# Decode block, forward and backward: row results as rows, and the query weight transposed as work of its own

## The chip, the cores and the metric

The kernel runs on one core of a Trainium2 chip. The metric is the device time of one execution in microseconds (us), the median of several. Lower is better.

## What is computed

The reference is the gradient step of a decode block for two tokens. Its forward part normalises `x`, adds an attention over a cached key/value store and a gated product network without activation function, and the backward part returns the gradients by every input but `B_x`:

```python
# B=2, Sq=1, D=576, Hq=32, Hkv=16, Sk=4096, Dh=128, F=4608, all bf16
def _A_ref(x, k_cache, v_cache, wq, wo):
    q = (x @ wq).reshape(B, Sq, Hq, Dh).transpose(0, 2, 1, 3)
    k, v = (jnp.repeat(c, 2, axis=1) for c in (k_cache, v_cache))
    p = softmax(jnp.einsum("bhqd,bhkd->bhqk", q, k) * Dh ** -0.5)
    o = jnp.einsum("bhqk,bhkd->bhqd", p, v)
    return o.transpose(0, 2, 1, 3).reshape(B, Sq, Hq * Dh) @ wo
def _B_ref(x, w_gate, w_up, w_down):
    return ((x @ w_gate) * (x @ w_up)) @ w_down
xn = layernorm(x)
out = x + _A_ref(xn, k_cache, v_cache, wq, wo) + _B_ref(xn, w_gate, w_up, w_down)
# outputs: out, and the vjp of out with grad_out: dx, dk, dv, dwq, dwo, dw_gate, dw_up, dw_down
```

`out_0` is the forward result and `out_1` is dx, two rows of 576 numbers each. `out_2` and `out_3` are the gradients of the caches, 32 MiB each. The others are the weight gradients.

## The kernel before

All inputs are read once and all outputs written once: some 92 MB each way.

**Steps and groups.** The 32 pairs of a batch row and a key/value head are worked through in 16 steps of two heads. Two steps (the two batch rows) make a group `g`, with a slice of 512 columns of `wq` and 512 rows of `wo`. A step loads two k and two v tiles of 1 MiB (`load_kv`), transposes them on DVE (`turn`), and computes the scores (L1268), the softmax, the contraction with v or k (L1442) and the outer products that are the gradients of v and k (`head_outer`, L1290; "pp" belongs to dv, "dd" to dk). `group_front` computes q and the gradient of the attention's output. `group_back` adds the group's part of the forward result to `acc`, and its part of the gradient by xn to `accx`. It also starts the units for the gradients of `wo` (`rows_unit`, L727) and of `wq` (`cols_unit`, L713, and `wide_unit`, L764, each with a tail of 64 rows, L826). `mlp` does the same for the nine slices of F.

**A unit** is a handful of products into a PSUM tile of two banks (`o`, three of them) and an eviction to a store tile on ACT or DVE (L470, L472). When all units of a store tile are done, `put` issues its store on SP (L696). All large loads and stores are issued by SP, which takes them in order and waits for each one's data and slot.

**Slots.** 16 tiles of 1 MiB (`big`) are shared by loaded tiles (`kv`), transposed ones (`X`), store tiles (`st`) and gate/up slices (`G`), each with a cap. There are five `ww` tiles for slices of `wq`, `wo` and `w_down`, and two PSUM tiles `m` of one bank for all small products.

**The order** of the instructions on every engine is fixed when the kernel is built. Generators yield what they need (`PE(...)`, `DVE(...)`, `ACQ` for a slot, `WAIT` for events). A planner (`Order`) advances them by estimated costs and takes, among those that are ready within `SLACK`, the one with the lowest priority number from `pr`. Tables of constants (`OFF`, `HEAD`, `TAIL`, `PR`, `MLP_AT`, `WQ_AT`, `WO_AT`) make these numbers, one for each kind of work and step.

**The ends of the rows.** `acc` holds the forward result in columns, 128 partitions by five pieces by two rows. `final_out` turns it into rows with nine fp32 products (L1504, L1507) behind two bf16 products that add `x` (`rows_add`, L1490). `rows_put` evicts with ACT and DVE and stores `out_0` with one DMA (L1486). `accx` holds partial sums of the gradient by xn, 144 columns on 128 partitions. `final_dx` sums it into columns with F8 (L1521, L1522), does the layer norm's gradient in columns with a mean product (L1530), adds `grad_out` (L1490), and turns the columns into rows with eight fp32 products (L1540, L1543). `front` prepares the columns of normalised `x` (`xnT`) with twenty small products (L650, L653).

Of the kernel before, what the change touches and what calls it, by code (L numbers as in the profile page):

```python
# [13 lines left out]
P = 128  # L14
# [276 lines left out]
def DMA(engine, cost, nbytes, row=8192):  # L291
# [7 lines left out]
OFF = {"turn0": {0: -1015.2, 1: -14.6, 2: -608.5, 3: -352.4, 4: -44.2, 5: -609.4, 6: 1026.5, 7: -575.3, 8: -336.9,  # L299
       9: -48.1, 10: 73.1, 12: 183.6, 13: 1140.9, 15: 354.0}, "turn1": {0: -158.8, 1: 373.8, 2: -399.3, 3: -123.5,  # L300
       4: -561.8, 5: 1792.7, 6: 184.6, 7: -225.4, 8: -1188.5, 9: -525.0, 10: -1211.4, 11: -134.5, 12: 1399.2, 13:
       -786.3, 14: 125.3, 15: -889.4}, "att": {0: -320.6, 1: 25.1, 2: -524.3, 3: 1437.6, 4: -1231.0, 5: 704.1, 6:
       -946.7, 7: -1656.2, 8: -1046.6, 9: 659.5, 10: -617.2, 11: -169.8, 12: 46.5, 13: -31.6, 14: -222.6, 15:
       1033.5}, "dsc": {0: -1811.3, 1: -9.9, 2: 131.1, 3: 301.3, 4: -3.2, 5: 235.2, 6: -975.3, 8: 26.8, 9: 229.2,
       10: -420.4, 11: 210.0, 12: 19.1, 13: 299.2, 14: 9.4}, "conv": {0: -2015.6, 1: 231.3, 2: -0.4, 3: -50.3, 4:
       -1165.8, 5: 1061.5, 6: 135.8, 7: 373.5, 8: -2359.6, 9: 3.5, 10: 1574.4, 11: 172.6, 12: 216.0, 13: 448.3, 14:
       255.6, 15: 10.6}, "con": {0: -32.2, 1: 1152.5, 2: 1696.5, 3: 720.8, 4: 638.1, 5: 104.8, 6: -260.9, 7: -158.3,
# [3 lines left out]
       9: -103.2, 10: -395.3, 11: 2850.9, 12: 125.0, 13: 2376.4, 15: -25.5}, "front": {0: -90.0, 1: 2844.9, 2:  # L311
       -805.5, 3: -966.7, 4: 1527.3, 5: 109.2, 6: 51.9, 7: -924.3, 8: -171.1, 9: -1466.9, 10: -796.2, 11: 95.0, 12:
       407.0, 13: 194.7, 14: 42.9, 15: -116.8}, "back": {0: -1180.5, 1: 591.1, 2: -2708.2, 3: 979.9, 4: 556.1, 5:
# [7 lines left out]
       13: -595.2, 14: -250.1, 15: 5.1}, "mlp": {0: 248.5, 1: 1168.1, 2: -620.3, 3: -398.1, 4: -321.8, 5: 2002.0, 6:  # L321
       162.1, 7: -3.7, 8: -33.1, 9: -2.4, 10: 1014.3, 11: 985.4, 12: 835.4, 13: -9.7, 14: 314.7, 15: -413.5},
       "load": {0: 1074.9, 1: -427.7, 2: 2940.0, 4: -302.0, 5: 501.3, 6: 157.2, 7: 2723.0, 8: 41.7, 9: 175.7, 10:
       -1207.2, 11: -514.7, 12: -5.8, 13: 248.9, 14: 607.8, 15: -253.7}, "wload": {0: -271.1, 1: 208.8, 2: -1828.2,
       3: 108.3, 4: 438.0, 5: -390.0, 6: 623.3, 7: 89.8, 8: -357.2, 9: -50.4, 10: 1806.6, 11: 48.4, 12: -1247.3, 13:
       3030.4, 14: 857.3, 15: 1037.7}, "mload": {0: 867.2, 1: -358.1, 2: -1319.2, 3: 100.2, 5: 58.5, 6: -3446.8, 9:
       -71.5, 10: -371.1, 11: -312.3, 12: 9.2, 13: 247.9, 14: 253.2, 15: -7.2}}
MLP_AT = [1.14, 5.4, 2.05, 2.45, 26.26, 69.69, 14.36, 0.0, 155.88]
WQ_AT = [-126, 9, 14, 22, -10, -36, 47, 13]
WO_AT = [-81, -88, -157, -95, 31, 1, -2, -56]  # L330
# [3 lines left out]
BIAS = 0.188  # L334
SLACK = {"PE": 0.06, "ACT": 0.25, "DVE": 0.4, "POOL": 10000.0, "SP": 10000.0}
STEP = 28.0
HEAD = {"turn0": -995.0, "turn1": -3790.2, "att": -3348.0, "dsc": 396.0, "conv": -832.5, "con": 1401.5, "out1":
        -1892.2, "out0": 2828.7, "front": 21.6, "back": 291.8, "W0": -1455.9, "W1": -155.0, "BD1": 1364.6, "BD0":
        2903.1, "mlp": 2389.4, "load": -3080.4, "wload": 394.7, "mload": -742.1}
TAIL = {"turn0": 3370.1, "turn1": 9221.8, "att": 665.4, "dsc": 359.0, "conv": 2694.5, "con": 2347.7, "out1": 7925.6,  # L340
        "out0": -1730.3, "front": 756.2, "back": 2986.8, "W0": 3398.4, "W1": -331.2, "BD1": -2581.8, "BD0": -508.7,
        "mlp": -5065.9, "load": 6824.2, "wload": 208.6, "mload": 3569.7}
PR = {"turn0": 1475.9, "turn1": 1614.7, "att": -4652.5, "dsc": -2890.4, "conv": 226.3, "con": -1413.1, "out1":
      3893.4, "out0": 2308.0, "front": 679.0, "back": 881.2, "W0": -1279.8, "W1": -624.6, "BD1": 2069.1, "BD0":
      -1551.4, "mlp": -735.6, "wout": -435.6, "store": -3305.7, "load": -1982.4, "wload": -3953.8, "fin": 5877.7,
      "const": 11595.3, "mload": -2275.6}
# [8 lines left out]
def kernel(  # L355
# [121 lines left out]
    nmu = const.tile([2, 1], FP32, name="nmu")  # L477
    warm = const.tile([1, 1], FP32, name="warm")
    rstd = const.tile([2, 1], FP32, name="rstd")
# [11 lines left out]
    meanc = filled("meanc", [P, 1], FP32, 1.0 / D)  # L491
    xnT = filled("xnT", [P, 16], FP32, 0.0)
    nrT = const.tile([P, 4], FP32, name="nrT")
    gg = const.tile([P, 2, 16], FP32, name="gg")
    gp4 = const.tile([P, 4], FP32, name="gp4")
    zero1 = filled("zero1", [P, 1], FP32, 0.0)
    acc = filled("acc", [P, 5, 2], FP32, 0.0)
# [17 lines left out]
    F8 = const.tile([P, 8], FP32, name="F8")  # L515
    Q4 = const.tile([P, 4], FP32, name="Q4")
# [1076 lines left out]
```

## Time and profile before

| | |
|---|---|
| median of 3 runs | 465.89 us (465.81 to 466.47) |
| profiled execution | 465.85 us, of which the span is 464.1 us |
| PE, DVE, ACT, POOL busy | 80%, 79%, 73%, 31% of the span |
| DMA | 185.97 MB, 401 GB/s over the span |
| mean granted PE clock | 0.70 of full speed |
| the 91 large stores (1024 and 576 KB), from issue to landing | 14.0 and 11.0 us (medians) |

The span is the time from the first to the last instruction of the profiled execution. Busy shares are averages over the whole span. An engine's busy time counts only where it ends last. The DMA line is the bytes that the 16 DMA engines moved. A line such as L470 is a helper's line: all plain evictions on ACT bear it, so the tile names say which work it was.

### The profile page before, as it was taken

The numbers are of one execution on the slowest core, as the hardware profiler recorded it, in microseconds if no ns is written. First come the engines' busy times: TensorE is split into PE (matmuls) and PEld (weight loads), VectorE is DVE, ScalarE is ACT, GpSimd is POOL, SyncE is SP. The second block draws the span as 40 slices with busy tenths as digits, with TensorE's granted clock in tenths as the row PEclk, the third lists the DMA queues.
The fourth block names the chain that finished last, engine by engine and source line by source line (L and its number), as shares of the span: only waits on it lengthen the run. The fifth ranks groups of instructions, "written<-read, shape, count | busy, mean of one in ns | idle before, by whom it ended". The sixth has DMA issues, their size and how long they took to land. (4 is left out here: it accounts for less than half of the span.)

```text
span 464.1 us, 15709 instructions
## 1 busy us (share of the span) xinstructions
PE 372.6 (80%) x6750; PEld 213.9 (46%) x6750; DVE 366.2 (79%) x708; ACT 337.7 (73%) x515; POOL 143.1 (31%) x174
## 2 busy tenths in 40 slices
PE   1677779789986877887887788879888987976995
PEld 1444455546443444454555354644543442533543
DVE  8897888876779887778987688977966887877782
ACT  3278639868886787765867778858857987897973
POOL 0740043303316443460016251140344463053000
PEclk9978776965557676756775796755666676586955
DMA  8999999999999999999999999999999999999994
GB/s 312 416 409 422 410 426 395 408 414 372 355 415 422 407 422 407 411 423 425 414 405 418 419 423 420 424 414 411 400 406 395 394 422 424 424 404 349 422 384 186
DMA packets 40710, 185.97 MB, mean 401 GB/s; under 512 B 3640, under 2 KB 12352, under 8 KB 24256
## 3 DMA queue, kind: packets, MB, share of 16 engines
q1 hardware_dynamic: 40632, 184.96, 98.7%
q8 instruction: 53, 0.87, 0.7%
q14 instruction: 17, 0.14, 0.1%
q10 hardware_dynamic: 8, 0.00, 0.0%
HBM read 92.48 MB, written 92.48 MB: 399 GB/s over the span
## 5 line engine op out<-in xcount | busy, mean ns | idle before, releaser
L470 ACT CAST big<-ps_o 128x1024 bf16<-128x1024 f32 (+2 forms) x309 | 278.9, 963 | 50.6 <-PE ps_o L1290 23.8
L466 DVE STREAM_TRANSPOSE big<-big 128x1024 f32<-128x1024 f32 x146 | 176.4, 1223 | 18.3 <-DMA big<-in_A_v_cache_dram 8.4
L1256 POOL TENSOR_TENSOR BD<-vr,mask 128x2048 bf16<-128x2048 bf16 x32 | 115.2, 3603 | 121.6 <-DVE vr L472 49.1
L472 DVE CAST big<-ps_o 128x1024 bf16<-128x1024 f32 (+1 forms) x69 | 73.4, 1065 | 17.8 <-PE ps_o L764 7.7
L1268 PE MATMUL ps_m<-big,W 128*32 128x128 bf16 x2048 | 57.3, 272 | 4.3 <-issue 1.8
L1233 POOL COPY W<-rep 32x16 bf16<-32x16 bf16 x128 | 24.6, 192 | 115.2 <-DVE rep L1007 99.2
L1268 PEld LDWEIGHTS <-W 128*32 128x32 bf16 x2048 | 45.5, 121 | 23.5 <-issue 22.5
L1290 PE MATMUL ps_o<-BD,dd 32*128 32x512 bf16 x256 | 45.8, 523 | 9.2 <-ACT big L470 5.6
L1290 PE MATMUL ps_o<-BD,pp 32*128 32x512 bf16 x256 | 44.5, 465 | 9.1 <-ACT big L470 7.5
L466 DVE STREAM_TRANSPOSE big<-ww 128x1152 f32<-128x1152 f32 (+1 forms) x25 | 33.0, 1318 | 3.5 <-DMA out_dram<-big 3.4
L1442 PE MATMUL ps_m<-big,dd 128*32 128x512 bf16 x256 | 30.7, 578 | 1.6 <-DVE dd L466 0.9
L1442 PE MATMUL ps_m<-big,pp 128*32 128x512 bf16 x256 | 29.2, 545 | 3.5 <-DVE pp L466 2.8
L1290 PEld LDWEIGHTS <-pp 32*128 32x128 bf16 x256 | 10.3, 95 | 29.3 <-issue 25.0
L1290 PEld LDWEIGHTS <-dd 32*128 32x128 bf16 x256 | 10.7, 99 | 26.3 <-issue 18.7
L764 PEld LDWEIGHTS <-xnr 32*128 32x128 bf16 x368 | 13.6, 119 | 14.3 <-issue 13.3
L764 PE MATMUL ps_o<-D,xnr 32*128 32x128 bf16 x256 | 14.7, 285 | 4.9 <-ACT big L470 3.6
L727 PE MATMUL ps_o<-dyr,R 32*32 32x288 bf16 x256 | 17.8, 406 | 0.8 <-ACT big L470 0.7
L1039 POOL COPY qr<-qd 128x256 bf16<-128x256 bf16 x8 | 3.2, 395 | 45.8 <-DVE qd L472 43.1
L727 PE MATMUL ps_o<-dyr,hb 32*32 32x288 bf16 x288 | 15.4, 327 | 1.7 <-ACT big L470 1.6
L888 PE MATMUL ps_m<-big,Wdy 128*128 128x128 bf16 x162 | 16.2, 278 | 0.4 <-DVE cr L1394 0.3
L678 PE MATMUL ps_m<-big,wm 128*32 128x128 bf16 x416 | 13.7, 294 | 2.6 <-DVE cr L1394 1.2
L888 PEld LDWEIGHTS <-Wdy 128*128 128x128 bf16 x162 | 14.4, 127 | 3.0 <-issue 2.7
(206 smaller groups left out, 481.6 us busy)
## 6 DMA issues: line engine op xcount, KB each, us to landing
out_dram<-big SPq DMA_DIRECT2D x74, 1024.0 KB, 14.0
big<-in_A_k_cache_dram SPq DMA_DIRECT2D x32, 1024.0 KB, 14.9
big<-in_A_v_cache_dram SPq DMA_DIRECT2D x32, 1024.0 KB, 13.6
out_dram<-big SPq DMA_DIRECT2D x17, 576.0 KB, 11.0
ww<-in_B_w_down_dram SPq DMA_DIRECT2D x9, 576.0 KB, 13.1
ww<-in_A_wo_dram SPq DMA_DIRECT2D x8, 576.0 KB, 10.9
ww<-in_A_wq_dram SPq DMA_DIRECT2D x8, 512.0 KB, 10.7
big<-in_B_w_gate_dram SPq DMA_DIRECT2D x4, 1024.0 KB, 14.5
```

Of the source, the lines that this page charges most:

```text
L466: nc.vector.transpose(out, in_)
L470: nc.scalar.copy(out, in_)
L472: nc.vector.tensor_copy(out=out, in_=in_)
L678: nc.tensor.matmul(dp[32 * q:32 * q + 32, 0:P], lhsT=W, rhs=view(X, 0, P, xoff(q, s), [[FS, 4], [2, 32]]), start=(s == 0), stop=(s == S - 1))
L727: nc.tensor.matmul(o[32 * q:32 * q + 32, aa, 0:HD2], lhsT=view(t, 32 * q, 32, 2 * A + aa, [[4, 32]]), rhs=dyr[32 * q:32 * q + 32, k * HD2: ...
L764: nc.tensor.matmul(o[:, aa, j * P:(j + 1) * P], lhsT=xnr[32 * a:32 * a + 32, dc * P:(dc + 1) * P], rhs=rhs(a), start=True, stop=True)
L888: nc.tensor.matmul(dh, lhsT=Wdy[:, e, 2 * k:2 * k + P], rhs=view(X[:], 0, P, 64 * k + e, [[D, FC], [2, 32]]), start=(k == 0 and e == 0), s ...
L1233: nc.gpsimd.tensor_copy(view(W_t[t][w][:], 32 * a, 32, 6 + 8 * a, [[G * WW, 4], [WW, G], [1, 2]]), view(rep_t[grp[g]["qs"]][:], 32 * a, 32 ...
L1256: nc.gpsimd.tensor_tensor(BD_t[i][:], view(vr_t[v][:], 0, P, 0, [[0, 16], [1, Dh]]), view(mask16[:], 0, P, 0, [[1, 16], [0, Dh]]), ALU.mult)
L1268: nc.tensor.matmul(sc[32 * cq:32 * cq + 32, :], lhsT=view(W[:], 0, P, (be * G + l) * WW + 6 - 4 * c2 - 2 * l, [[1, 32]]), rhs=view(X[:], 0 ...
L1290: nc.tensor.matmul(o[:, k, :], lhsT=pr2[32 * c4:32 * c4 + 32, :], rhs=BD[32 * c4:32 * c4 + 32, 8 * l + 4 * h2:8 * l + 4 * h2 + 4, :], star ...
L1442: nc.tensor.matmul(ct[32 * j:32 * j + 32, :], lhsT=view(rT, 0, P, 4 * c + 2 * l, [[1, 32]]), rhs=kv_t[kvS[s][t][l]][:, Dh * c:Dh * (c + 4) ...
```

## The change

Three things change together.

1. **Rows.** `acc` changes its layout from pieces by rows to rows by pieces, so that one fp32 product with the identity gives ten rows of 128 numbers: `final_out` is that product, one DVE addition of `x` (kept in the same form, `xrow`), and four stores. `final_dx` sums `accx` into eight rows of 144 numbers with one product, does the layer norm's gradient on DVE in that form (with one small product for the means), and stores it with three DMAs whose pieces are 64 and 32 bytes long. `front` prepares `x` and `grad_out` in these forms with 21 bf16 products and one fp32 product. `final_out` has a priority of its own (`finy`).
2. **Transposes of `wq`.** The two DVE transposes of a group's `wq` slice leave `group_back` and form a generator of their own, `turn_wq`, with priorities `wqt`. It waits for the group's `Ed` and for the `spread` of its second step, takes an `X` slot, and gives the `ww` tile back. `group_back` waits for `Ewqt`.
3. **The order.** All tables of constants are new, and `BIAS` and `SLACK` (the planner's preference of ACT for evictions, and its window of choice) with them. The planner's other costs are as they were.

The diff without the tables:

```diff
-BIAS = 0.188
-SLACK = {"PE": 0.06, "ACT": 0.25, "DVE": 0.4, "POOL": 10000.0, "SP": 10000.0}
+BIAS = 0.117
+SLACK = {"PE": 0.06, "ACT": 0.26, "DVE": 0.32, "POOL": 10000.0, "SP": 10000.0}
...
-    acc = filled("acc", [P, 5, 2], FP32, 0.0)
+    acc = filled("acc", [P, 2, 5], FP32, 0.0)
...
     # front(): preparation of the row forms
-            for c in range(4):
-                nc.tensor.matmul(tp[32 * c:32 * c + 32, 2 * a:2 * a + 2], lhsT=xb[:, P * c + 32 * a:P * c + 32 * a + 32],
-                                 rhs=ident[0:2, 0:2], start=True, stop=True)
...
+        for dc in range(5):
+            nc.tensor.matmul(tp[0:10, 288:416], lhsT=Zw[:, 4 - dc:14 - dc], rhs=xb[:, DOFF[dc]:DOFF[dc] + P],
+                             start=(dc == 0), stop=(dc == 4))
...
+        for n in range(2):
+            row = xy[0:2, n * D:(n + 1) * D]
+            for a in range(4):
+                nc.tensor.matmul(tp[0:8, 144 * n:144 * n + P], lhsT=Zw[:, 3 - a:11 - a],
+                                 rhs=view(row, 0, 2, 32 * a, [[P, 4], [1, 32]]), start=(a == 0), stop=(a == 3))
...
+        nc.vector.tensor_copy(xrow, tp[0:10, 288:416])
+        nc.vector.tensor_copy(grow, tp[0:8, 144:288])
+        nc.vector.tensor_copy(nr8, tp[0:8, 416:418])
+        nc.vector.tensor_scalar(xn8, tp[0:8, 0:144], nr8[:, 0:1], nr8[:, 1:2], op0=ALU.add, op1=ALU.mult)
+        nc.vector.tensor_scalar(nrs, nr8[:, 1:2], -1.0, None, op0=ALU.mult)
...
+    def turn_wq():
+        for g in range(NG):
+            st = grp[g]
+            yield PRIO(pr("wqt", 2 * g))
+            yield WAIT(st["Ed"], steps[2 * g + 1]["spread"])
+            wq = ww_t[st["wq"]]
+            x = st["wqt"] = yield ACQ("X")
+            X = X_t[x]
+            yield DVE(1.25)
+            t32(pairs(X[:, 0:4 * FS]), pairs(wq[:, 0:4 * FS]))
+            yield REL("ww", st["wq"])
+            yield DVE(0.4)
+            t32(pairs(X[:, 4 * FS:5 * FS]), pairs(tq[:, FS * (g % 4):FS * (g % 4 + 1)]))
+            yield SET(st["Ewqt"])
...
     # group_back(g)
-        x = yield ACQ("X")
+        yield WAIT(st["Ewqt"])
+        x = st["wqt"]
         X = X_t[x]
-        yield DVE(1.25)
-        t32(pairs(X[:, 0:4 * FS]), pairs(wq[:, 0:4 * FS]))
-        yield REL("ww", st["wq"])
-        yield DVE(0.4)
-        t32(pairs(X[:, 4 * FS:5 * FS]), pairs(tq[:, FS * (g % 4):FS * (g % 4 + 1)]))
...
     def final_out():
-        yield PRIO(PR["fin"])
+        yield PRIO(PR["finy"])
         yield WAIT(Eprep, *acc_E)
-        i = yield ACQ("o")
...
-        yield from rows_put(o, 0, out_0)
-        yield REL("o", i)
+        i = yield ACQ("m")
+        yt = m_t[i][0:10, 0:P]
+        yield PE(0.0, 0.4)
+        nc.tensor.matmul(yt, lhsT=acc[:].rearrange("p b k -> p (b k)"), rhs=identf[:], start=True, stop=True)
+        yield DVE(0.25)
+        nc.vector.tensor_tensor(yrow, yt, xrow, ALU.add)
+        yield REL("m", i)
+        rows = out_0.rearrange("b s d -> (b s) d")
+        for b in range(2):
+            yield DMA("SP", 0.3, 1024, 256)
+            nc.sync.dma_start(rows[b, 0:512].rearrange("(c n) -> c n", c=4), yrow[5 * b:5 * b + 4, :])
+            yield DMA("SP", 0.3, 128, 128)
+            nc.sync.dma_start(rows[b:b + 1, 512:576], yrow[5 * b + 4:5 * b + 5, 64:P])
 
     def final_dx():
...
+        g8, mt = m_t[i][0:8, 0:144], m_t[i][0:8, 144:146]
+        yield PE(0.0, 0.5)
+        nc.tensor.matmul(g8, lhsT=F8[:], rhs=accx[:], start=True, stop=True)
+        yield DVE(0.6)
+        nc.vector.reduce_sum(s8[:, 0:1], g8, axis=AX.X)
+        nc.vector.tensor_tensor_reduce(out=t8, in0=xn8, in1=g8, scale=1.0, scalar=0.0, op0=ALU.mult, op1=ALU.add,
+                                       accum_out=s8[:, 1:2])
         yield PE(0.0, 0.1)
+        nc.tensor.matmul(mt, lhsT=M8[:], rhs=s8, start=True, stop=True)
+        yield DVE(0.9)
+        nc.vector.tensor_copy(m8, mt)
+        nc.vector.scalar_tensor_tensor(out=t8, in0=xn8, scalar=m8[:, 1:2], in1=g8, op0=ALU.mult, op1=ALU.subtract)
+        nc.vector.tensor_scalar(t8, t8, m8[:, 0:1], nrs, op0=ALU.add, op1=ALU.mult)
+        nc.vector.tensor_tensor(dxrow, t8, grow, ALU.add)
+        yield REL("m", i)
+        rows = out_1.rearrange("b s d -> (b s) d")
+        for b in range(2):
+            yield DMA("SP", 0.3, 1024, 64)
+            nc.sync.dma_start(rows[b, 0:512].rearrange("(c a j) -> a c j", a=4, j=32),
+                              dxrow[4 * b:4 * b + 4, 0:P].rearrange("a (c j) -> a c j", j=32))
+        yield DMA("SP", 0.3, 256, 32)
+        nc.sync.dma_start(rows[:, 512:576].rearrange("b (a j) -> b a j", a=4), dxrow[0:8, P:144])
```

More of the change, by code (lines that the diff above doesn't have):

```diff
@@ L655, in front @@
-        nc.tensor.matmul(bp, lhsT=view(ones[:], 0, 2, 0, [[0, P]]), rhs=nr, start=True, stop=True)
-        yield DVE(0.9)
-        nc.vector.tensor_copy(xnT[:, 0:8], tp[:, 0:8])
-        nc.vector.tensor_copy(xnT[0:16, 8:16], tp[0:16, 8:16])
-        nc.vector.tensor_copy(nrT[:], bp)
-        for k, op in ((0, ALU.add), (2, ALU.mult)):
-            nc.vector.tensor_tensor(xnT[:], xnT[:], view(nrT[:], 0, P, k, [[0, 8], [1, 2]]), op)
-        nc.vector.memset(gg[:, 0], 0.0)
+        tp = m_t[i]
@@ new lines, in front @@
+        yield PE(0.0, 0.6)
+        for dc in range(5):
+            nc.tensor.matmul(tp[0:10, 288:416], lhsT=Zw[:, 4 - dc:14 - dc], rhs=xb[:, DOFF[dc]:DOFF[dc] + P],
+                             start=(dc == 0), stop=(dc == 4))
+        yield DVE(0.2)
+        nc.vector.memset(Zw[:], 0.0)
+        nc.vector.tensor_copy(view(Zw[:], 0, 2, 3, [[4, 2]]), ident[0:2, 0:2])
+        yield PE(0.0, 1.2)
+        for n in range(2):
[3 more added lines that the diff above has]
+                                 rhs=view(row, 0, 2, 32 * a, [[P, 4], [1, 32]]), start=(a == 0), stop=(a == 3))
+            for a in range(4):
+                nc.tensor.matmul(tp[0:8, 144 * n + P:144 * n + 144], lhsT=Zw[:, 3 - a:11 - a],
+                                 rhs=row[:, 512 + 16 * a:528 + 16 * a], start=(a == 0), stop=(a == 3))
@@ L971, in mlp @@
         yield REL("hb", hs)
[L974 removed]
+    grp = [dict(Lm=Event(), Eq=Event(), Ed=Event(), Lo=Event(), EoT=Event(), Ewqt=Event()) for _ in range(NG)]
     Lq = events(2)
@@ L1527, in final_dx @@
-        nc.vector.tensor_tensor(gx, g, xnT[:], ALU.mult)
-        nc.vector.reduce_sum(gp4[:], view(gg[:], 0, P, 0, [[16, 2], [1, 2], [2, 8]]), axis=AX.X)
-        yield PE(0.0, 0.1)
-        nc.tensor.matmul(mt[:, 16:20], lhsT=view(meanc[:], 0, P, 0, [[0, P]]), rhs=gp4[:], start=True, stop=True)
-        yield DVE(0.5)
-        mean = [view(mt[:], 0, P, 16 + 2 * k, [[0, 8], [1, 2]]) for k in range(2)]
-        nc.vector.tensor_tensor(gx, xnT[:], mean[1], ALU.mult)
-        nc.vector.tensor_tensor(gx, g, gx, ALU.subtract)
```

179 lines of the change are left out of this document (68 added, 111 removed), and 21 rows, old and new, of the table OFF.

## The prediction, made before the changed kernel was run

> **What bounds the kernel now.** I read the page's slices first, then the busy time by stretch, then SP's issues in order of time, then the chain that ended last.
>
> ```profile
> PEclk9978776965557676756775796755666676586955
> DMA  8999999999999999999999999999999999999994
> GB/s 312 416 409 422 410 426 395 408 414 372 355 415 422 407 422 407 411 423 425 414 405 418 419 423 420 424 414 411 400 406 395 394 422 424 424 404 349 422 384 186
> ```
>
> The 16 DMA engines are busy nearly throughout, at 400 to 426 GB/s, and the bytes do not change. So time is lost only where these engines run dry. The last slice (186 GB/s) is the largest such place. The stretches show the others (columns: us, busy time and count on PE, PE weight loads, DVE, ACT and POOL, granted clock, DMA share, GB/s):
>
> ```profile
> 112.00:114.00 2.00, 2.00 (x54) 1.43 (x48) 1.59 (x4) 1.99 (x3) 0.09 (x1) 0.50 0.67 263
> 418.00:420.00 2.00, 1.17 (x37) 0.71 (x35) 0.00 (x0) 2.00 (x3) 0.00 (x0) 1.00 0.61 232
> 448.00:450.00 2.00, 2.00 (x25) 0.93 (x25) 1.49 (x5) 1.44 (x2) 0.00 (x0) 0.50 0.76 281
> 456.00:458.00 2.00, 1.11 (x10) 0.71 (x5) 0.69 (x4) 1.01 (x1) 0.00 (x0) 0.50 0.30 91
> 460.00:462.00 2.00, 0.00 (x0) 0.00 (x0) 0.03 (x1) 0.26 (x1) 0.00 (x0) 0.50 0.08 29
> ```
>
> One minus the DMA share, times the length, is idle time. Over 112 to 116 it is 0.66 + 0.48 = 1.1 us, over 416 to 420 0.16 + 0.78 = 0.9 us: some 2.1 us in mid-kernel. From 446 to the end, in the same 2 us stretches, it is 0.48 + 0.20 + 1.40 + 0.40 + 1.84 + 2.03 = 6.4 us. In that tail PE works without a pause at half clock (6.00 of 6.00 us between 448 and 454; ACT 3.07, DVE 3.30). PE is therefore late there, and the stores with it:
>
> ```profile
> 449.29 0.56 PE ps_o L1490 x2
> 449.86 1.80 PE ps_o L1504 x16
> 451.65 0.30 PE ps_o L1507 x2
> 451.95 1.08 PE ps_o L727 x12
> ...
> 454.46 0.53 PE ps_m L1521 x2
> 454.99 0.15 PE ps_m L1522 x2
> 455.14 0.56 PE ps_o L1490 x2
> 455.70 0.54 PE ps_o L713 x8
> ...
> 457.65 1.87 PE ps_o L1540 x8
> ```
>
> This is the chain (start, us, what). The products of `final_out` stand ahead of the rows units (L727) that feed the last three large stores, and the first products of `final_dx` stand between the two units (L713) of the very last one.
>
> ```profile
> 457.32 0.38 SPq L696 DMA_DIRECT2D out_dram<-big  x1
> 460.29 0.26 SPq L1486 DMA_DIRECT2D out_dram<-xy  x1
> ```
>
> The last line is `out_1`, issued last. It does not end last: SP's final wait (L1588) is put down to `out_dram<-big`, 2.3 us, and by the packet records `out_1` is moved at 461.0 while the last 1 KB piece of the large store ends at 462.7, 1.4 us before the end. So the store issued at 457.32 sets the end, and a shorter `final_dx` gains nothing unless that store also comes earlier.
>
> **The change, part by part.** Sums are made against the profiled execution, 465.85 us = span 464.07 + 1.78, which is the median (465.89) but for 0.04.
>
> *`final_out` on PE.* Removed: 0.56 + 1.80 + 0.30 = 2.66 us. Added: one fp32 product of 128 columns; the four such products of L1540 take 1.87 us, so 0.47 each. The removed work lies on the path to the last store: -2.19 us.
>
> *`final_dx` before its last unit.* 0.53 + 0.15 + 0.56 = 1.24 us stand between the two last units. In the new order the F8 product comes behind all sixteen products of these units: -1.24 us. Together the last large store moves by 3.43 us, from 457.32 to 453.9.
>
> *What is late next.* DMA: the stretches from 446 on move 4.52 MB, which at 415 GB/s take 10.9 us; with 1.4 us to the end that floor is 458.3, below 464.07 - 3.43 = 460.64. ACT and DVE are half idle there. So the store stays the end.
>
> *The rest of `final_dx`.* It must end below 460.64. The last units now end on PE at 456.24 - 3.43 = 452.8; DVE evicts its half of the last store first (1.2 us), to 454.0. Then a reduction over 144 columns (0.30, as the 128x144 add L1111), the multiply with sum (0.29 + 0.08, L1386), the fp32 mean product (0.53, L1530), a copy (0.15), three passes over 144 columns (0.35 as L1397, then 0.30 and 0.27) and 0.3 for seven hand-overs of 0.02 to 0.05: 2.6 us, to 456.6. Three issues of 0.3 us: the third begins at 457.2. Its packets follow 0.75 us later (460.29 to 461.05 now), and 1.4 us close: 459.4. Hidden, by 1.2 us; beyond that it costs its excess.
>
> The trace holds no store in 64 and 32 byte pieces; its nearest row is the 1152 byte row at 0.05 us a packet, against 0.009 us for a 4 byte semaphore write, so 40 pieces on 16 engines cost 0.03 to 0.15 us. The Trainium skill (DMA: Bandwidth & Descriptors, Specifications) says that transfers under 512 B are read, modified and written, and its latency section gives up to 2 us for one access under load. By that, as an estimate, `final_dx` would end at 461.4 instead of 459.4 and the time would be 463.2; no row here shows it, and the sum does not use it.
>
> The PE terms are taken at the tail's granted 0.50. The Trainium skill (TensorE: Matmul & The Clock Gate, What's actually happening) says that 3.4 us of sustained work release full clock. The trace disagrees: PE is busy 6.00 of 6.00 us at 0.50. By the rule the removed work would be worth about half, 1.7 us, and the time 464.1.
>
> *Four stores for `out_0`.* Three more SP issues, 0.9 us, ahead of the last three large stores. SP is idle between 452.75 and 453.81, which covers them; uncovered, +0.9.
>
> *Preparation.* DVE has 12 small instructions in place of 11, two of them wider (0.3 each): +0.5 us between 12 and 17 us, before waits for PE of 0.68, 0.56 and 0.26 us, while the queue holds loads only (first store at 30.22). Zero; uncovered, +0.5.
>
> *`turn_wq`.* The same transposes (1.2 + 0.40 us a group), taken out of `group_back` and put ahead. In the tail they run at 449.6 to 451.2, with the product that needs them at 452.96: not on the path, so zero. It holds one of the 16 big slots for longer; a load that then waits is late by about a transpose, up to 1.6 us.
>
> *The order.* SP's first 17 loads are the same in both orders. After that all differs. By SP's list, the last v load stands 1.0 MiB later (162.2 behind 161.2), about 2.5 us, and 14.2 MiB follow it instead of 15.2. PE has by then done more: behind the last dp scores 6 instead of 14 pp products (L1290, 0.30 each) and none instead of 16 (L1442, 0.12 each) remain, 4.4 us less. That covers the 2.5 us. The first of the last dK stores stands 9.3 MiB (23.5 us) behind that load, 12.0 before; from the landing (by 423.04) to that store (about 446) it took 23 us, so the cover is thin. Over the other steps the least such distances are 10.0 and 11.2 (before 12.9 and 13.2), 25 us and more. For mid-kernel I take no change; its bounds are -2.1 us (all idle gone) and the loss of the second rival.
>
> Sum: 465.85 - 2.19 - 1.24 = 462.4 us.
>
> **The rivals.** *More than the tail:* the new order also loses the idle of 112 to 116 and 416 to 420: 462.4 - 2.1 = 460.3. For it: the fourth gate/up slice is spread out (its down load stands at 42.1 MiB, not 31.4), and the first stall came in a stretch where PE was busy 6.00 of 6.00. Against: every order so dense must stall somewhere.
>
> *Slower:* SP takes its queue in order, so a store whose evictions are late holds up the loads behind it, and once DMA's backlog of about 10 us (14 us to landing less 4 for an empty queue, my estimate) is spent, DMA runs dry. Before, two wide stores of `grads` took SP from 111.0 to 117.0, and DMA lost 1.1 us. In the new order four of them stand in a row, two v loads behind them, and only 10.0 MiB after the down load they depend on (12.0 before). At the same pace they take 12 us, 6 us more with the backlog already spent: 462.4 + 6 = 468.4. It decides from 4.4 us of added idle. Against: the slice's PE work is no longer bunched with the three others.
>
> *It does not reach the end:* the last store's path shortens, but a later v load, thin cover at the last dK stores or a straggling DMA engine gives 3 us back: about 465.4.
>
> **How the numbers follow.** A difference of under 0.2% (0.93 us) can't be told from no change. Forecast, 461 to 464.5: 0.50. More than the tail: 0.15. Given back: 0.11. Slower: 0.24. Faster is 0.65, same 0.11, slower 0.24. The range goes from 459.0 (the first rival, and 1.3 for the spread of DMA rates) to 468.5 (the second).
>
> **What would show it.** Right: `final_out` one product of about 0.5 us; from the last rows units to the last large store no fp32 products on PE; idle DMA after 446 of about 3 us; SP's last wait still for `out_dram<-big`. Wrong: a slice in mid-kernel under 340 GB/s, above all around the four wide stores in a row; or SP's last wait for `out_dram<-xy`, which would mean that the small pieces end last; or a tail in which PE idles and evictions or loads are late.

## Result and profile after

The changed kernel takes 471.53 us (median of 6 runs, 470.41 to 471.73) beside 466.39 us for the kernel before on the same chip (6 runs, 465.81 to 466.74): 5.1 us slower, ratio 1.0106 (95% interval 1.0091 to 1.012). The profiled execution took 471.39 us, its span 469.6. The slices of the page after (DMA share in tenths, GB/s; 11.7 us each):

```profile
DMA  8999999999999999999999999999999999998994
GB/s 319 413 410 364 382 420 412 411 419 419 407 396 395 391 426 409 422 420 418 402 378 422 419 359 410 401 415 330 421 423 419 423 422 419 423 402 327 421 391 161
```

The bytes are the same, 185.97 MB. Two slices in mid-kernel lie under 340 GB/s (330 near 323 us, 327 near 429), the first of the signs that the prediction named for being wrong. The last slice is lower than before's (161, 186 before). By 450 us the changed kernel had moved less than the kernel before; first before, then after, the DMA view of the first 450 us:

```profile
DMA packets 39603, 182.78 MB, mean 406 GB/s; under 512 B 3551, under 2 KB 11611, under 8 KB 23380
```

```profile
DMA packets 38326, 181.12 MB, mean 402 GB/s; under 512 B 3473, under 2 KB 10453, under 8 KB 22101
```

1.66 MB at the prediction's 415 GB/s are 4.0 us: most of the 5.5 us between the spans is lost ahead of the tail. Stretches after (columns as in the prediction):

```profile
40.00:42.00 2.00, 1.66 (x11) 0.80 (x13) 2.00 (x4) 2.00 (x5) 0.00 (x0) 1.00 0.67 279
...
318.00:320.00 2.00, 1.54 (x42) 0.90 (x30) 2.00 (x3) 1.63 (x3) 2.00 (x1) 0.50 0.72 288
424.00:426.00 2.00, 2.00 (x45) 1.03 (x41) 1.43 (x3) 1.68 (x2) 1.95 (x1) 0.50 0.77 281
426.00:428.00 2.00, 1.79 (x23) 0.63 (x20) 1.55 (x4) 1.32 (x3) 0.00 (x0) 0.93 0.50 134
...
460.00:462.00 2.00, 0.46 (x4) 0.10 (x2) 1.68 (x6) 0.71 (x1) 0.00 (x0) 0.50 0.10 38
462.00:464.00 2.00, 0.00 (x0) 0.00 (x0) 0.89 (x3) 0.00 (x0) 0.00 (x0) 0.50 0.10 35
```

The stall of 112 to 116 is gone. That of 416 to 420 has only moved, to 424 to 428: before, an SP issue behind the last gate and up slice took 5.05 us at 414.01, and now one behind the same slice takes 4.99 us at 421.97. Others have come near 41, 275 and 319 us. Idle time is not all of the loss. Summed over stretches of 2 us from 2 to 450 us, the mean DMA engine idles 5.2 us before and 6.9 after, 1.6 us more. Its packets also took longer: 14.4 us in all above the commonest duration of their size (309 ns for 8 KiB), 12.0 before. What lengthens them stays open.

In the tail PE is done at 460.3 but for one small product, and the DMA engines stand nearly empty from 460 to 464. The DMA share there, 0.10, is hardly more than one engine of 16 (0.06). That number is the key to the case, as the experiments show.

The PE part of the change did what was said. PE in the tail after (start, us, instructions):

```profile
456.11 0.60 PE L1513 MATMUL ps_m<-identf,acc 128*10 128x128 f32 x2
459.05 0.63 PE L729 MATMUL ps_o<-Q,xnr 32*128 32x128 bf16 x16
459.62 0.65 PE L1530 MATMUL ps_m<-accx,F 128*8 128x144 f32 x2
```

`final_out` is one product of 0.60 us, and the product with F8 stands behind all sixteen of the last two units. SP in the tail after (start, duration; L1520 and L1522 are `out_0`'s four stores, L1546 and L1549 `out_1`'s three):

```profile
457.12 0.49 SPq L1520 DMA_DIRECT2D out_dram<-xy  x1
458.61 0.24 SPq L1522 DMA_DIRECT2D out_dram<-xy  x1
461.35 0.25 SPq L1520 DMA_DIRECT2D out_dram<-xy  x1
462.77 0.23 SPq L1522 DMA_DIRECT2D out_dram<-xy  x1
463.11 0.37 SPq L712 DMA_DIRECT2D out_dram<-big  x1
...
464.46 0.45 SPq L712 DMA_DIRECT2D out_dram<-big  x1
465.74 0.72 SPq L1546 DMA_DIRECT2D out_dram<-xy  x2
466.51 0.71 SPq L1549 DMA_DIRECT2D out_dram<-xy  x1
```

Four stores of 2.3 KB in all spread over 5.7 us, and the last large store, whose evictions end at 461.0, is issued at 464.46. SP's waits after say why (us in total, times, longest):

```profile
SPq L1520 <- DMA out_dram<-big: 2.5, 1, 2.5
SPq L1522 <- DMA out_dram<-big: 2.1, 2, 1.2
SPq L1591 <- DMA out_dram<-xy: 0.9, 1, 0.9
```

An issue waits for the landing of the transfer eight back on the same queue; here those are large stores. A landing is recorded once for each DMA engine, and these records say more. When SP issued the small store at 461.35 and the large one at 464.46, the transfer eight back had been down on fifteen engines since 456.29 and 459.63 us; the sixteenth followed at 461.33 and 464.39. So one late engine holds SP here. The last wait is for `out_dram<-xy`, the second of the signs for being wrong.

### The profile page after: what moved, and what is told of

Its sections match the earlier page's. It is cut to its first block, busy times and chain, and to the rows that moved or that the text cites. A ratio compares the mean times of both kernels' runs of the same rounds, so it can differ in the third digit from the quotient of the medians.

```text
span 469.6 us, 15669 instructions
## 1 busy us (share of the span) xinstructions
PE 377.8 (80%) x6713; PEld 215.0 (46%) x6713; DVE 369.7 (79%) x701; ACT 335.6 (71%) x519; POOL 143.4 (31%) x174
## 2 busy tenths in 40 slices
DMA packets 40772, 185.97 MB, mean 396 GB/s; under 512 B 3706, under 2 KB 12414, under 8 KB 24318
## 4 chain that ended last, share of the span: by engine, by line
DMA 46%; PE 25%; DVE 14%; ACT 9%; issue 3%; POOL 1%; SPq 0%; ACTq 0%; DVEq 0%; POOLq 0%
DMA out_dram<-big 16%; DMA big<-in_A_v_cache_dram 15%; ACT big L475 7%; DVE big L471 7%; PE ps_o L1317 4%; DMA ww<-in_B_w_down_dram 4%; PE ps_m L1469 4%; DMA big<-in_A_k_cache_dram 4%; PE ps_m L1295 4%; DMA ww<-in_A_wq_dram 3%; PE ps_o L743 3%; DMA ww<-in_A_wo_dram 3%; DVE big L477 3%; PE ps_m L904 1%; DMA xy<-in_grad_out_dram 1%
## 5 line engine op out<-in xcount | busy, mean ns | idle before, releaser
L477 DVE CAST big<-ps_o 128x1024 bf16<-128x1024 f32 (+2 forms) x68 | 75.2, 1107 | 11.5 <-PE ps_o L743 2.5
L1295 PE MATMUL ps_m<-big,W 128*32 128x128 bf16 x2048 | 63.7, 294 | 4.8 <-DVE sp L477 1.0
L1295 PEld LDWEIGHTS <-W 128*32 128x32 bf16 x2048 | 50.9, 132 | 26.7 <-issue 25.9
L1317 PE MATMUL ps_o<-BD,pp 32*128 32x512 bf16 x256 | 48.4, 493 | 8.5 <-ACT big L475 7.6
L1469 PE MATMUL ps_m<-big,dd 128*32 128x512 bf16 x256 | 28.7, 538 | 0.7 <-DVE oT L1489 0.3
L1479 ACT ACTIVATE osb<-ps_m 128x512 bf16<-128x512 f32 x15 | 9.0, 600 | 14.3 <-PE ps_m L1469 11.7
L1039 PE MATMUL ps_m<-big,Wdy 128*128 128x128 bf16 x144 | 13.8, 272 | 4.6 <-DVE cr L1421 2.7
L475 ACT CAST osb<-ps_m 128x512 bf16<-128x512 f32 x15 | 8.9, 593 | 11.5 <-PE ps_m L1469 11.1
L780 PEld LDWEIGHTS <-xnr 32*128 32x128 bf16 x368 | 11.1, 114 | 10.2 <-issue 9.5
```

The source lines that it names most:

```text
L475: nc.scalar.copy(out, in_)
L477: nc.vector.tensor_copy(out=out, in_=in_)
L780: nc.tensor.matmul(o[:, aa, j * P:(j + 1) * P], lhsT=xnr[32 * a:32 * a + 32, dc * P:(dc + 1) * P], rhs=rhs(a), start=True, stop=True)
L1039: nc.tensor.matmul(dp, lhsT=Wdy[:, e, 2 * k:2 * k + P], rhs=view(X[:], 0, P, 64 * k + e, [[D, GH], [2, 32]]), start=(k == 0 and e == 0), s ...
L1295: nc.tensor.matmul(sc[32 * cq:32 * cq + 32, :], lhsT=view(W[:], 0, P, (be * G + l) * WW + 6 - 4 * c2 - 2 * l, [[1, 32]]), rhs=view(X[:], 0 ...
L1317: nc.tensor.matmul(o[:, k, :], lhsT=pr2[32 * c4:32 * c4 + 32, :], rhs=BD[32 * c4:32 * c4 + 32, 8 * l + 4 * h2:8 * l + 4 * h2 + 4, :], star ...
```

## Experiments

Theories at the start. **T1:** the row results gain in the tail as worked out, the eight in flight on SP give it back, and the new order costs more in the middle. **T2:** all of the loss is `out_0`'s small stores in the tail. A third came up on the way. **T3:** the work on PE in the tail never set the end; one late DMA engine did.

**Out_0's stores from POOL.** The changed kernel, L1520 and L1522:

```diff
-            nc.sync.dma_start(rows[b, 0:512]...
+            nc.gpsimd.dma_start(rows[b, 0:512]...
```

> The changed kernel with one edit: the four small stores of out_0 are issued by POOL instead of SP, at the same place in the order. Theory (SP's queue): in the changed kernel SP issues the four at 457.12, 458.61, 461.35 and 462.77 us, each of the last three waiting for a large store several issues back to land, and the last large store, whose evictions end at 461.02, is issued only at 464.46; so without them on SP it is issued by 461.3, out_1 at about 463.0 instead of 465.74, and the time falls by 2.7 to 3.4 us, to 468.0 to 468.8. Rival (the loss lies in mid-kernel alone, in idle DMA time before 430 us): the tail has slack of its own, and the time stays within 0.5 us of 471.5.

471.02 us (469.1 to 472.02); ratio 1.0095 [1.0063, 1.0127]. The issue part held: the last large store went out at 461.98, just behind its evictions. The end did not move: span 470.2. A stretch of this run:

```profile
466.00:468.00 2.00, 0.00 (x0) 0.00 (x0) 0.00 (x0) 0.00 (x0) 0.00 (x0) 0.50 0.06 24
```

A share of 0.06 is one engine of 16. In the packet records fifteen engines end by 465.1, one at 468.75. T2 falls; T3 begins here.

**Rows alone.** The kernel before with the row results of the change (`acc`, `front`, `final_out`, `final_dx`) and the planner's costs, tables and order exactly as before; no `turn_wq`.

> The kernel before with the row results alone: its own tables, its own order on every engine, transposes of wq where they were; only final_out, final_dx and their preparation are the new ones, with four and three small stores on SP (the first product of final_dx behind the last unit). Theory (the PE sum of the prediction holds, and the loss comes with the new order): the last large store comes 2 to 3.4 us earlier than 457.3, and the time is 462.4 to 464.0. In this order the issues eight back of the small stores are mostly small or old ones, so SP should lose under 1 us to them. Rival (the small stores cost as much in any order): SP is held for about 4 us, and the time is 466 to 467.5. Second rival (mid-kernel): no difference before 440 us between this run and the kernel before beyond 0.5 us; if there is one, the preparation in the front disturbs the order's timing.

466.53 us (466.07 to 467.7), ratio 1.0003 [0.9986, 1.002]: no change. So the row results cost and gain nothing at a fixed order, and the loss comes with the new order and `turn_wq`. SP held the last large store to 458.56 here as well, and one engine alone was at work to 463.41.

**Tables.** The changed code with the tables of before (priorities `finy` and `wqt` as after), and the code before with the tables of after.

> The changed kernel's code with the tables, BIAS and SLACK of the kernel before (only the two entries that it lacks, finy and wqt, taken from the new ones), so that the planner finds yet another order. Theory (an order made by numbers that were not found for the code at hand loses in mid-kernel): 468 to 478, with idle DMA time before 430 us of 5 us or more. Rival (the tables of before are simply the better ones, and what is added by wqt costs nothing): 463 to 466.

> The kernel before, its code unchanged, with the new tables, BIAS and SLACK. Theory (as for the run with the tables of before in the new code): 468 to 478. Rival (the new tables are worse in themselves by what the changed kernel loses in mid-kernel, about 5 us, whatever the code): 470 to 472.

479.65 us (ratio 1.0285) and 475.9 us (1.0205), two runs each. Either set of numbers costs 10 to 13 us on code for which it was not found. So neither set can be judged apart from its code, and the share of `turn_wq` can't be told from that of the order by exchanging them.

**Small stores taken out of SP's way**, at before's order (all seven from POOL; or `out_0`'s four on SP, but behind the last large store), and in the changed kernel (`out_0`'s four behind the last large store). The edit is a move of the four `dma_start` lines from `final_out` to `final_dx`, or `sync` to `gpsimd`.

> Before's order and before's code but for the row results, as in the run with the rows alone; here all seven small stores (four for out_0, three for out_1) are issued by POOL instead of SP. Theory (the products gain about 3 us and the small stores on SP give them away, since SP's issues wait for the DMA eight back to land): the last large store is issued within 0.3 us of its last eviction, near 456 us, out_1's stores near 457.5 to 459, and the time is 462.5 to 464.5 us. Rival (the end is not set by the issue but by one DMA engine that runs behind the other 15, whatever the order of the issues): the last large store is issued as early, and the time stays at 465.8 to 467.

> As the run with the rows alone, all on SP, but out_0's four small stores are issued behind the last large store, just ahead of out_1's three. Theory (eight in flight on SP): the last large store is issued within 0.6 us of its last eviction, out_1's issues still wait for small and large stores to land, and the time is 463 to 465 us. Rival (a late DMA engine sets the end): 465.8 to 467 us, with the large store issued early all the same. Second rival (small stores are dear wherever they stand on SP): 465.5 to 467 us with out_1's last issue later than 460 us.

> The changed kernel with out_0's four small stores issued behind the last large store, everything else and the order of the rest as it was. Theory: out_5's last store is issued near 459 us and the last large store near 461.1 us instead of 464.46, and the time is 468.5 to 470.0 us: still above the kernel before, because the order in the middle of the kernel is dearer by 3 to 5 us. Rival (the whole loss lies in the tail): 466 to 467 us. Second rival (a late DMA engine sets the end): 471 to 472 us.

468.11 us [1.0024, 1.0052], 467.75 us [1.0011, 1.0037] and 470.91 us [1.007, 1.0114]: the first two are slower than the kernel before, by 1.8 and 1.5 us, which is not explained, and the third lies within the interval of the changed kernel. In the first (profiled in its fastest run, 466.72 us) the last large store went out 2.4 us earlier than in the kernel before (457.32 there):

```profile
454.93 0.38 SPq L705 DMA_DIRECT2D out_dram<-big  x1
```

```profile
458.00:460.00 2.00, 0.00 (x0) 0.00 (x0) 0.00 (x0) 0.00 (x0) 0.37 (x1) 0.50 0.15 32
460.00:462.00 2.00, 0.00 (x0) 0.00 (x0) 0.00 (x0) 0.00 (x0) 0.00 (x0) 0.50 0.06 25
```

Everything else is done by 459, and one engine works alone to 463.39. In the records of landings, this engine's part of each DMA lands later and later behind the next latest: 0.3 to 1.0 us near 240 us, 2.3 to 2.5 near 375, 4.3 to 4.8 near 450 in the kernel before, and 4.5 to 5 near 450 in the changed kernel and in the variants. From 1.8 us to the last packet of a large store there is no moment at which no engine is at work, in the kernel before, in the changed one, and in these. T1's expected gain of the tail fix (468.5 to 470.0 for the last of the three) fell with this; its dearer order stands.

**The last gate and up slice from POOL**, on top of `out_0`'s stores late, to take away a stall near 416 to 420 us (an SP issue of 5 us):

> As the run with the rows alone and out_0's stores behind the last large one, and the last slice of gate and up (512 columns, two loads of 512 packets of 1 KB) is issued by POOL instead of SP. Theory (SP's next issue stands about 5 us behind these two loads while the DMA engines run dry for 0.9 us): no SP issue between 405 and 425 us takes longer than 1.5 us, no 1 us stretch there is without packets, and the time is 0.5 to 1.5 us under the same kernel with all its loads on SP. Rival (the 5 us are the ring's own and move with the loads to POOL, or POOL's own issue costs as much): no difference within 0.4 us, or up to 2 us slower.

467.56 us [1.0014, 1.0037], as without. The stall did go: no issue of 405 to 425 us took over 0.87 us, and the DMA share was 1.00 to 1.01 from 412 to 420 (0.61 at 418 to 420 before). Filling the mean engine's gap gained nothing, which T3 says and T1 does not.

**Load moved between the engines.** First, two 1 MiB stores as 120 and 8 rows, in three kernels (before; rows with POOL; after with late stores):

```diff
-            nc.sync.dma_start(d, x)
+                nc.sync.dma_start(d[0:120], x[0:120])
+                nc.sync.dma_start(d[120:P], x[120:P])
```

> The kernel before, in which two of the large stores (1 MiB, 128 rows of 8192 bytes, issued near 285 and 350 us) are each issued as two: 120 rows, and the 8 rows left. In every run so far one of the 16 DMA engines falls slowly behind: a DMA's last landing comes 4.5 to 5 us behind the one before it at 450 us, and that engine is alone at work for the last microseconds (456.9 to 458.2 and 460.3 to 462.7 in the kernel before). By the Trainium skill (DMA: Bandwidth & Descriptors, Why a DMA increments its semaphore by 16 and not by 1) a DMA from SP goes to the lowest-numbered k of the 16 engines, k the largest number up to 16 that divides its rows: 15 for 120 rows, 8 for 8. Theory (the late engine sets the end, and it is the one that 120 rows leave out): it is spared 8 packets of 309 ns by each of the two, 4.9 us in all; its landings at 450 us come with those of the others, and the time falls by 1.5 to 4 us, to 462.5 to 465, until the chain of final_dx sets the end. Rival (the late engine sets the end but is another one): no change within 0.5 us, the lag still 4.5 to 5 us. Second rival (the work on PE and the order of the issues set the end, the late engine doesn't): the lag shrinks and the time stays within 0.5 us.

> Before's order with the row results new, all small stores from POOL, and two of the large stores issued as 120 and 8 rows. Without the split it took 468.1 us, with the last large store issued at 454.9 us and all DMA engines but one done by 459. Theory (late engine, and the one that 120 rows leave out): the late engine's end moves from 463.4 us to about 459.5, and the time falls to 462 to 464.5: the row products then gain what the late engine hid. Rival (another engine is late): 467.5 to 468.5, the lag as before. Second rival (the small stores from POOL set the end): lag gone, 466.5 to 468.

> The changed kernel with out_0's stores behind the last large store, and two of the large stores issued as 120 and 8 rows. Without the split it took 470.9 us, all DMA engines but one done by 462.9 and that one at 467.1. Theory (late engine, the one that 120 rows leave out): 466.5 to 468.5 us; what stays above the kernel before is the order in the middle. Rival (another engine is late): 470 to 471.5 us.

469.0 us (466.9 to 470.14; ratio [1.0033, 1.0074]), 468.67 [1.0036, 1.0079] and 472.79 [1.0125, 1.0168]. The lag did not shrink; in the first it rose to 6.5 us. So the late engine is not the one that 120 rows leave out. If it is one of the eight that take the 8 rows, it got 0.6 us more; the rest of the 2.7 us of the first is unexplained, though its lag was 3.0 us at 288 us, before the first split store had landed, where the kernel before had 1.2.

Then the last 576 and 512 KiB stores as 119 and 9 rows, in the kernel before and in rows with late stores:

> The kernel before, in which the last 576 KiB store and the last 512 KiB store are each issued as 119 rows and 9 rows. By the same section of the Trainium skill 119 rows go to the lowest 7 engines (17 rows each) and 9 rows to the lowest 9, so that the other engines are spared nearly all of 8 packets of 178 ns and 32 of 46 ns, 2.9 us. Theory (a late engine outside the lowest 7 sets the end): the time falls by 1 to 2 us, to 464.3 to 465.3. Rival (the late engine is among the lowest 7): 468.5 to 470 us. Second rival (the late engine does not set the end): 466 to 467.

> Before's order with the row results new, out_0's four stores behind the last large one, and the last 576 KiB and 512 KiB stores issued as 119 and 9 rows. Without these it took 467.75 us with the late engine alone at work from 459.8 to 464. Theory (a late engine outside the lowest 7 sets the end): 464 to 465.5 us, under the kernel before, since the row products' 3 us are no longer hidden. Rival (it is among the lowest 7): 470 to 471. Second rival (the late engine does not set the end): 467 to 468.

471.72 us [1.0092, 1.013] and 474.56 us [1.015, 1.0195]: slower by 5.2 and, against the same kernel without, 6.8. The late engine's chain of packets now holds 17 + 1 of 4608 bytes and 68 + 4 of 1024, so it is one of the seven that got 17 rows in place of 8. That is 10 x 178 ns and 40 x 46 ns more, 3.6 us of load on it and on six others. Only this one engine is late with it (first run):

```profile
464.00:466.00 2.00, 0.00 (x0) 0.00 (x0) 0.00 (x0) 0.00 (x0) 0.00 (x0) 0.50 0.12 39
466.00:468.00 2.00, 0.00 (x0) 0.00 (x0) 0.00 (x0) 0.00 (x0) 0.00 (x0) 0.50 0.07 24
```

3.6 us more of load on this engine made 5.2 us more of time; the 1.6 us between them are not explained. The Trainium skill (DMA: Bandwidth & Descriptors, Why a DMA increments its semaphore by 16 and not by 1) says that a DMA uses the lowest-numbered k engines, k the largest number up to 16 that divides its rows. The 17-packet chain and a count of 4-byte packets that rose by 14 with the two 120 + 8 splits (15 + 8 in place of 16, twice) agree with it. A variant meant to put a store on eight engines left that count as it was (3636), so it changed nothing and serves as a control:

> The kernel before, in which the last 1 MiB store (issued near 450 us) is written as 8 runs of DRAM instead of 128 rows, the same bytes to the same places. By the Trainium skill (DMA: Bandwidth & Descriptors, Why a DMA increments its semaphore by 16 and not by 1) such a DMA uses only the lowest 8 of the 16 DMA engines; a count of 4-byte packets lower by 8 than the kernel before's would show it. Then the lower half gets 8 packets of 309 ns more each (2.5 us) and the upper half 2.5 us less. In the kernel before one engine is 4.5 to 4.8 us behind at 450 us. Theory A (the late engine sets the end and lies in the upper half): the end moves 1.5 to 2.5 us earlier, to 464 to 465 us. Theory B (it sets the end and lies in the lower half, outside the four that the pieces of 64 bytes used): 2 to 2.5 us later, 468.3 to 469. Rival (the late engine does not set the end): within 0.5 us of before.

466.3 us, ratio 0.9998 [0.9987, 1.0009].

**More work on PE in the tail.** The kernel before, `final_out`'s eleven products twice:

```diff
-        rows_add(o, 0)
-        for dc in range(5): ...
+        for again in range(2):
+            rows_add(o, 0)
+            for dc in range(5): ...
```

> The kernel before with final_out's products done twice, one group behind the other into the same bank: 2.66 us more of TensorE ahead of the last two units, nothing else changed. Theory (one DMA engine that is behind sets the end, and reaches the last large store only at about 460.6 us, 2.7 us after its issue at 457.9): the last large store is issued 2.5 us later, and the time grows by 0 to 1 us. Rival (the chain of work on PE in the last 20 us sets the end, as the chain of waits of the kernel before reads, and as the prediction had it): the time grows by 2 to 2.7 us, to 468.3 to 469.

466.97 us beside 466.25, ratio 1.0016 [1.0002, 1.0029]: +0.7 us for 2.66 us of PE. The last large store came 2.4 us later, and that was all:

```profile
459.75 0.38 SPq L696 DMA_DIRECT2D out_dram<-big  x1
```

So the kernel before has some 2 us of room on PE in its tail (1.3 to 2.6 by the interval); the prediction had none.

**What makes the engine late.** Transfers alone, then with TensorE instructions beside them (none computes the reference's outputs). The body of the first:

```python
for i in range(64 + 5):
    if i < 64: nc.sync.dma_start(big[i % 12][:], at(ins, i))
    if i >= 5: nc.sync.dma_start(at(outs, i - 5), big[(i - 5) % 12][:])
# the other two, ahead of it: 6600 or 3300 times
nc.tensor.matmul(acc[:], lhsT=w[:], rhs=w[:], start=True, stop=True)
```

> No computation at all: 64 loads of 1 MiB (all of the two caches) and 64 stores of what was loaded, from SP, twelve buffers, and nothing on the other engines; its outputs are not the reference's. By 309 ns for a packet of 8192 bytes the span is near 320 us. Theory (one engine falls behind by what the stream itself does to it): a DMA's last landing comes 3 to 4 us behind the one before it at the end. Rival (what falls on one engine is the fetching of instructions, 53 packets of 16 KiB in the kernel before, or the 17 of 8 KiB on the other instruction queue): the lag stays under 0.5 us throughout.

> The bare stream of 128 transfers again, with 6600 products of 32 x 32 on TensorE beside it (13,200 instructions with their weight loads, about as many as the kernel before has, which shows 53 packets of 16 KiB on the instruction queue); all of one small tile of zeros, waiting for nothing, and its outputs are not the reference's. In the stream without them no DMA engine was ever more than 0.5 us behind the next. By the Trainium skill (NeuronCore Runtime (NRT), Instruction fetch mechanics) instructions are fetched in blocks of 16 KiB by a DMA queue, mostly hidden. Theory (the fetching of TensorE's instructions falls on one engine more than on the others and makes it late): about 50 packets of 16 KiB, and the lag of the last landing grows to 3 to 6 us by the time the products are done. Rival (fetching is spread evenly, and the lag has another cause: the mixture of packet sizes, the waits between the transfers, or the traffic of the engines): the lag stays under 1 us.

> The same with 3300 products instead of 6600; outputs as little the reference's. Theory: about 25 packets of 16 KiB and half the lag of the other, 1.5 to 3 us. Rival: the lag under 1 us in both.

322.09, 338.4 and 329.48 us, one run each, the first on another chip than the other two. Of the run with 6600 products, then of that with 3300, the instruction queue's line (packets, MB, share) and a late stretch or two (columns: busy on PE, PE weight loads, DVE, POOL, granted clock, DMA share, GB/s):

```profile
q8 instruction: 51, 0.84, 0.9%
...
328.00:332.00 4.00, 0.00 (x0) 0.00 (x0) 0.00 (x0) 0.00 (x0) 1.00 0.06 27
```

```profile
q8 instruction: 25, 0.41, 0.4%
...
320.00:324.00 4.00, 0.00 (x0) 0.00 (x0) 0.00 (x0) 0.00 (x0) 1.00 0.32 135
324.00:328.00 4.00, 0.00 (x0) 0.00 (x0) 0.00 (x0) 0.00 (x0) 1.00 0.04 16
```

Without products the lag is never over 0.53 us, and 0.16 at the end. With 25 packets of 16 KiB it grows to 3.2 us while they are fetched (to 154 us), lies between 1.7 and 2.7 after that, and is 2.7 at the end; with 51 it reaches 8.4 and is 7.2 at the end. The slowest engine ends at 319.2, 326.5 and 335.4 us: 0.29 and 0.32 us more for each packet. The products wait for nothing and nothing waits for them. This is shown: TensorE's instructions make one DMA engine late, in proportion to their number. The Trainium skill (the page is titled Runtime: NRT & Kernel Launch; Instruction fetch mechanics) calls the cost of crossing into the next 16 KiB block mostly hidden. Here the run with 51 blocks took 16.3 us longer, though nothing waited for the products.

That the fetching itself does it is not shown. In the run with 3300 products, from 87 to 160 us, the late engine's landings come 4.3 us later in all than at its usual 2.45 us a DMA. Packets that took 330 to 420 ns instead of 309 make up 4.2 us of that, and all 67 of them lie between 3.7 us ahead of the start of a recorded 16 KiB packet and 0.1 us behind it. The 16 KiB packets show elsewhere: the data packet that starts as one of them ends takes 0.67 to 0.86 us, every time, and the late engine's landings have no such delay then. So what slows the late engine comes once for each block of instructions, but it can be another part of the fetch or other traffic that goes with the instructions, such as the profiler's own records of them. No run separates these, and none has TensorE's instructions taken out of the kernel itself.

## Why the prediction was wrong, step by step

- ***What is late next*: the step that failed.** The floor of 458.3 us was a mean over 16 engines. The floor is that of the slowest one. Its part of the data, packets at their commonest durations, is 446.0 us; 53 packets of instructions, at the 0.29 to 0.32 us of the two streams, add 15.4 to 17.0, an estimate of 461.4 to 463.0 us. Measured are 461.0 us, from 1.75 to this engine's last packet at 462.71; with 1.4 us to the end that is the span itself. That the two agree so well is in part luck, since the estimate leaves out the 12 us by which the mean engine's packets exceeded their commonest durations. What shows that this engine sets the end are three runs: 2.66 us more of PE cost 0.7, a last store issued 2.4 us earlier gained nothing, and 3.6 us more of load on this engine cost 5.2. "So the store stays the end" was read rightly, as the last piece to land, but what it waited for was this engine's queue and not its own issue.
- ***final_out* and *final_dx* on PE (-2.19, -1.24): right in kind, worth nothing.** The new product of `final_out` took 0.60 us instead of 0.47, the one with F8 stood behind the last units as forecast (0.65 us), and the last large store did come earlier, by 2.4 us of the 3.43 where SP did not hold it. The rows alone changed the time by a factor of 1.0003 [0.9986, 1.002].
- ***The rest of final_dx*:** 2.0 us from the first reduction to the row (460.93 to 462.96), 2.6 expected. Its issues came later than 457.2 even at before's order (461.0), held by SP's eight in flight.
- ***Small pieces*:** the 32 pieces of 64 bytes landed within 0.16 us (467.36 to 467.52 after). The extra 2 us that the prediction gave as an estimate beside its sum do not show.
- ***The clock*:** granted 0.50 after too, from 452 us on, PE busy 2.00 of 2.00 us at 456 to 458.
- ***Four stores for out_0*: wrong in mechanism.** Not three issues of 0.3 us under idle time of SP, but waits for the transfer eight back, 3.4 us on the last large store, and in the end for the late engine's part of it. Price in the changed kernel: about 0.6 us, within the spread (471.53 against 470.91), since the late engine had work until about then.
- ***The order*: the second step that failed.** "No change in mid-kernel" was taken from distances in SP's list. The stalls came elsewhere. SP's waits of 34 to 43 and of 262 to 276 us after:

```profile
SPq L712 <- ACT big L475: 5.6, 1, 5.6
```

```profile
SPq L712 <- ACT big L475: 6.4, 1, 6.4
SPq L1170 <- DMA out_dram<-big: 4.5, 1, 4.5
```

  A store whose eviction on ACT is late holds SP for 5.6 or 6.4 us, and a load behind it then waits 4.5 us for a slot that a store must free. That is how the rival *Slower* works, but not at its place: at the four wide stores in a row (141 to 167 us) the DMA engines hardly paused (shares of 1.01 to 1.05). That such waits make the loss is likely but not shown. The kernel before has them too (whole run, us in total, times, longest):

```profile
SPq L696 <- ACT big L470: 94.8, 52, 5.2
SPq L696 <- DVE big L472: 61.0, 27, 5.4
```

  The added idle time is only 1.6 us, and the longer packets have no cause on record. What is shown is the sum. With 52 instruction packets in both, the late engine ended at 468.27 us in the changed kernel and at 463.41 where before's order ran the same rows: 4.9 us, the size of the whole loss (5.1), and not by more instructions.
- ***Preparation* and *turn_wq*:** not measured by themselves. The share of `turn_wq` in the loss, with the tile it holds for longer, stays open: order and transposes come out of one plan.
- **The sum.** 465.85 - 3.43 should have been 465.85 - 0 + about 5 for the order. The rivals had the stall (468.4) and "a straggling DMA engine" (465.4) but as accidents, and not together.

None of the versions here beats the kernel before.

## What to carry to other kernels

Work out the DMA floor from the slowest engine: a DMA share of 0.06 ahead of the end means that one engine of 16 is alone at work, and then, as here, a shorter tail on PE or a filled gap of the others can gain nothing. Test slack by making the suspected work dearer before making it cheaper; one run with `final_out` doubled would have shown that it was not on the path. Numbers of a planner belong to the code they were found for. TensorE instructions are not free to the DMA engines: in the two streams every 260 of them (one packet of 16 KiB) went with 0.3 us on the slowest engine. Whether a kernel with fewer of them is faster was not tried.

## What the hardware showed that was not expected

- One DMA engine is later than the rest in proportion to TensorE's instructions: 0.2, 2.7 and 7.2 us at the end for 0, 25 and 51 packets of 16 KiB, and 7.4 and 16.3 us of time. The recorded packets of 16 KiB are not what delays it.
- SP holds an issue until its transfer eight back has landed: up to 2.5 us for a store of 1 KB behind large ones. Where it was looked up, fifteen engines had landed it 4.8 to 5.1 us earlier, so that the late one held SP. From POOL the same stores are not held.
- An SP issue behind the last gate and up slice (2 x 512 packets of 1 KiB) took 5.05 us at 414.0 in the kernel before, while the other engines ran dry (DMA share 0.61). The changed kernel has the same behind that slice, 4.99 us at 421.97. With these two loads on POOL none took over 0.87 us. What holds the issue was not tried by itself.
